# Second mixture: the second product by Strassen's algorithm in passes 1 and 2, with prepared weights kept in DRAM

## Chip, cores and metric

The kernel runs on one core of a Trainium2 chip. The metric is the device time of one execution in microseconds (us); lower is better. Engines are named TensorE (PE, its weight loads PEld), VectorE (DVE), ScalarE (ACT), GpSimd (POOL) and SyncE (SP, which issues nearly all DMAs here).

## The reference, cut to what matters

Attention with positive features gives x (2304 tokens by 512); a first mixture routes each token to one of 8 experts; the second mixture, below, sends every token through all 8 experts and weights them with a normalised gate P.

```python
def _moe2_ref(x, w_gate, w1, w2):          # x 2304x512, E = 8, F = 1024
    logits = x @ w_gate
    P = np.exp(logits - logits.max())
    for _ in range(8):
        P /= P.sum(1, keepdims=True) + 1e-09
        P /= P.sum(0, keepdims=True) + 1e-09
        P *= N / E
    out = np.zeros((N, D))
    for e in range(E):
        h = np.maximum(x @ w1[e], 0.0)
        out += P[:, e:e + 1] * (h @ w2[e])
    return out
```

## The kernel before

Attention and the first mixture come first; the second mixture (`moe2`) starts near 420 us of the span and is all that the change touches. Every fp32 operand is split into a high part, rounded to fp32r by ScalarE, and a low part, the rest, made by VectorE; a product is three matmuls, high by high, high by low and low by high.

The tokens are done in three passes of 768 (two halves of three 128-token tiles, `TB` = 3, `TW` = 384). In a pass the 8 experts' weights come in 16 parts of 512 hidden units; one part in one pass is a *quad*, 48 in all, 16 a pass, in reversed order every other pass. A quad has two groups (`group`, L1127), each for half of its hidden units.

The **first product** (x by w1) is done by Strassen's algorithm on 2x2 blocks: seven products for eight. `sums_w1` (L865) makes the sums of weight blocks on GpSimd, `w1_high` and `w1_low` (L879, L885) split the seven operands, `sum_x`, `x_high` and `x_low` do so for x once a pass. `mm` (L1069) issues one product: 6 matmuls of 384 columns. They add up in the PSUM tiles `pa`, `pb`, `pd` with a few VectorE sums (L1146, L1161, L1173), and `relu_high`, `relu_low` (L1087, L1095) leave the split activations.

The **second product** (activations by w2) is done plainly, a quad later: `piece` (L1101) takes one 128-token tile and issues 12 matmuls of 512 columns into `py`; VectorE multiplies by the gate and accumulates (L1123). `load_w2`, `w2_high`, `w2_low` (L1052 to L1065) bring the quad's four 128-row parts of w2 through two raw buffers. Weights are loaded, summed and split anew in every pass.

The gates are made in the first quads (`sinkhorn_start`, `sinkhorn_step`). From quad 3 (`AUTO`) on the order is the one written (`manual_schedule`, L1261): each engine runs its instructions in program order. `group` takes lists `high`, `low` and `fill`, which put the preparation of the next weights and the pieces of the quad before between the products. All loads and stores of `moe2` stand in the one SP queue, in program order.

Of the kernel before, what the change touches and what calls it, by code (L numbers as in the profile page):

```python
# [18 lines left out]
P = 128  # L19
# [794 lines left out]
def moe2(tc, nc, c, w_gate, w1, w2, x2d, xtd, out):  # L814
# [6 lines left out]
    with ExitStack() as ctx:  # L821
# [6 lines left out]
        ORDER = (1, 6, 7, 2, 5, 3, 4)  # L828
        AUTO = 3
        yield  # L830
        wp = ctx.enter_context(tc.tile_pool(name="m2w", bufs=1, reuse_waits="tile"))
        weights = [(e, q) for e in range(E) for q in range(NQ)]
        quads = []
# [9 lines left out]
        wc, wsrc = {}, {}  # L843

        def load_w1(m):

            if m >= len(wlist):
                return
            e, q = wlist[m]
            r = wp.tile([P, NKB, 2, QF], F32, name="r1", tag="r1")  # L850
            for h in range(2):
                nc.sync.dma_start(
                    r[:, :, h],
                    w1[e, :, 512 * h + QF * q : 512 * h + QF * q + QF].rearrange("(b p) f -> p b f", p=P),
                )
            wsrc[m] = r

        def views_w1(m):
            r = wsrc[m]
            a11, a12, a21, a22 = r[:, 0:2, 0], r[:, 2:4, 0], r[:, 0:2, 1], r[:, 2:4, 1]  # L860
            s1 = wp.tile([P, 2, QF], F32, name="s1", tag="s1")
            s2 = wp.tile([P, 2, QF], F32, name="s2", tag="s2")
            wsrc[m] = {1: a11, 6: s2, 2: a12, 7: a21, 5: s1, 3: a12, 4: a22}

        def sums_w1(m):  # L865
            if m:
                views_w1(m)
            a11, s2, a12, a21, s1, _, a22 = wsrc[m].values()
# [7 lines left out]
        def w1_tiles(m, k):  # L876
            wc[m, ORDER[k]] = [wp.tile([P, 2, QF], F32R, name=nm, tag=nm, bufs=7) for nm in ("wch", "wcl")]

        def w1_high(m, k):  # L879
            i = ORDER[k]  # L880
            if (m, i) not in wc:
                w1_tiles(m, k)
            nc.scalar.activation(wc[m, i][0], wsrc[m][i], AF.Copy)  # L883

        def w1_low(m, k):  # L885
            i = ORDER[k]
            src = wsrc[m]
            h, l = wc[m, i]
            nc.vector.tensor_tensor(l, src[i], f32(h), ALU.subtract)  # L889
            if i == 2 and m:  # L890
                nc.gpsimd.tensor_tensor(src[3], src[2], src[6], ALU.subtract)  # L891

        load_w1(0)
        views_w1(0)
        for k in range(7):
            w1_tiles(0, k)

        for k in (0, 3, 6, 1, 2, 4, 5):
            yield
# [27 lines left out]
        def load_x(t, tag="xr", bufs=2):  # L927
            xr = big.tile([P, D], F32, name="xr", tag=tag, bufs=bufs)
# [24 lines left out]
        def other_logits(ps_, h):  # L953
            xt = big.tile([P, NKB, TW], F32, name="xt", tag="xt")
            for i, t in enumerate(tiles(ps_, h)):
                transposed(load_x(t), lambda pt: [(xt[:, :, i * P : i * P + P], pt)])
# [11 lines left out]

        def new_x():
            for h in range(2):  # L970
                for kh in range(2):
                    xq[h, kh] = big.tile([P, 2, TW], F32, name="xq", tag="xq", bufs=4)
# [12 lines left out]
        xs, xc = {}, {}  # L985

        def sum_x(i, first=False):
            b11, b12, b21, b22 = xq[0, 0], xq[1, 0], xq[0, 1], xq[1, 1]
            v = nc.vector
            if i == 0:  # L990

                d = big.tile([P, NKB, TW], F32, name="xt", tag="xt")[:, 0:2] if first else b12
# [23 lines left out]
        def sum_4():  # L1016
            nc.vector.tensor_tensor(xs[4], xs[2], xs[6], ALU.subtract)
# [31 lines left out]
        hs = {}  # L1049
        w2s, w2r = {}, {}  # L1050

        def load_w2(m, b):  # L1052
            if m >= len(wlist):
# [15 lines left out]
        def mm(dst, n, g, i, start, stop):  # L1069
            wh, wl = wc[wid[n], i]  # L1070
            xh, xl = xc[i]
            sl = slice(g * P, g * P + P)
            m = 0
            for w, x in ((wh, xh), (wh, xl), (wl, xh)):
                for kb in range(2):
                    nc.tensor.matmul(  # L1076
                        dst, w[:, kb, sl], x[:, kb], start=(start and m == 0), stop=(stop and m == 5),
# [9 lines left out]
        def relu_high(n, g, half, which, src):  # L1087
            hh, hl = [
                big.tile([P, TW], F32R, name=f"{nm}{half}", tag=f"{nm}{half}", bufs=6 + 2 * half)
                for nm in ("hh", "hl")  # L1090
            ]
            nc.scalar.activation(hh, src, AF.Relu)  # L1092
            hs[n, 2 * g + which, half] = (hh, hl)
# [7 lines left out]
        def piece(n, half, i):  # L1101

            ps_, e, q = quads[n]
            k = n % len(weights)
# [3 lines left out]
            for b in range(4):  # L1108
                hh, hl = hs[n, b, half]
                wh, wl = w2s[wid[n], b]  # L1110
                for ht, wt in ((hh, wh), (hl, wh), (hh, wl)):
                    nc.tensor.matmul(py, ht[:, i * P : i * P + P], wt, start=(m == 0), stop=(m == 11))  # L1112
                    m += 1
            if k == 0:
                accs[t] = big.tile([P, D], F32, name="acc", tag="acc", bufs=2 * TB)
                if ps_ == 0:
                    nc.scalar.activation(accs[t], py, AF.Copy)
                else:
                    nc.scalar.activation(accs[t], py, AF.Copy, scale=lg[:, t, e : e + 1])
            elif k < NQ and ps_ == 0:  # L1120
# [3 lines left out]
            if k == len(weights) - 1:  # L1124
                nc.sync.dma_start(row(t, 1), accs[t])

        def group(n, g, fill, high, low, lead=()):  # L1127
# [16 lines left out]
            mm(b, n, g, 6, True, False)  # L1144
# [4 lines left out]
            mm(d, n, g, 7, True, False)  # L1149
# [8 lines left out]
            mm(b, n, g, 5, False, False)  # L1158
# [8 lines left out]
            mm(b, n, g, 3, False, True)  # L1167
            relu_high(n, g, 1, 0, b)
            relu_low(n, g, 1, 0, b)
            mm(d, n, g, 4, False, True)  # L1170
# [12 lines left out]
        xrs = [[load_x(t, "acc", 2 * TB) for t in tiles(0, h)] for h in range(2)]  # L1183
        for h in range(2):
            for i, t in enumerate(tiles(0, h)):
                x_block(xrs[h][i], h, i)
            if h == 0:
                xs.update({1: xq[0, 0], 2: xq[0, 1]})
                for k in (0, 3):
                    x_high(k)  # L1190
                    x_low(k, True)
        for i in range(3):
            sum_x(i, True)
            if i:
                x_high(i)
                x_low(i)
        sum_4()
        for k in (4, 5, 6):
            x_high(k)
            x_low(k)  # L1200
        others = [(ps_, h) for ps_ in range(1, NPASS) for h in range(2)]
        load_w2(0, 0)
        load_w2(0, 1)
# [166 lines left out]
```

## Time and profile before

| | before |
|---|---|
| three runs, us | 1963.07, 1967.33, 1971.89 (median 1967.33) |
| profiled execution, us | 1964.43 |
| its span, us | 1962.4, 32469 instructions |
| PE, DVE, ACT, POOL busy | 98%, 63%, 45%, 17% |
| mean granted clock of PE | 0.995 of full speed |
| DMA | 180.78 MB, mean 92 GB/s |

The span runs from the first to the last instruction; the rest of the profiled execution's time lies around it. Busy shares are of the whole span. A matmul's duration in the trace overlaps that of the next, so the distance between starts tells its rate.

### The profile page before, as it was taken

The numbers are of one execution on the slowest core, as the hardware profiler recorded it, in microseconds if no ns is written. First come the engines' busy times: TensorE is split into PE (matmuls) and PEld (weight loads), VectorE is DVE, ScalarE is ACT, GpSimd is POOL, SyncE is SP. The second block draws the span as 40 slices with busy tenths as digits, with TensorE's granted clock in tenths as the row PEclk, the third lists the DMA queues.
The fourth block names the chain that finished last, engine by engine and source line by source line (L and its number), as shares of the span: only waits on it lengthen the run. The fifth ranks groups of instructions, "written<-read, shape, count | busy, mean of one in ns | idle before, by whom it ended". The sixth has DMA issues, their size and how long they took to land.

```text
span 1962.4 us, 32469 instructions
## 1 busy us (share of the span) xinstructions
PE 1932.2 (98%) x12594; PEld 1732.4 (88%) x12594; DVE 1230.8 (63%) x2189; ACT 889.2 (45%) x1682; POOL 328.0 (17%) x294
## 2 busy tenths in 40 slices
PE   9999899989999999999999999999999999999999
PEld 8988889966889989899998989989998999999997
DVE  5777777764866656666655666565665656656563
ACT  5777555545444344344344434344444434444341
POOL 2011532211111111112021111111201111111110
PEclk9999999989999999999999999999999999999999
DMA  6324686545122121222122121222202122121211
GB/s 180 105 64 112 162 305 221 205 126 170 65 65 71 59 75 54 81 84 72 68 62 76 54 82 54 81 72 90 76 35 92 54 80 73 56 76 54 83 47 43
DMA packets 132550, 180.78 MB, mean 92 GB/s; under 512 B 22370, under 2 KB 86114, under 8 KB 132384
## 3 DMA queue, kind: packets, MB, share of 16 engines
q1 hardware_dynamic: 128768, 171.22, 28.4%
q0 software_dynamic: 3456, 7.30, 1.0%
q8 instruction: 101, 1.65, 0.4%
q14 instruction: 65, 0.53, 0.1%
q10 hardware_dynamic: 160, 0.07, 0.0%
HBM read 163.85 MB, written 17.15 MB: 92 GB/s over the span
## 4 chain that ended last, share of the span: by engine, by line
PE 77%; DVE 0%; DMA 0%; ACT 0%; issue 0%; SPq 0%; ACTq 0%
PE py L1112 40%; PE pb L1076 15%; PE pa L1076 10%; PE pd L1076 10%; PE pg L944 1%; PE pt L936 1%; DMA xr<-x2d 0%; ACT acc L1260 0%; DVE w2l L1067 0%; PE pl L949 0%; PE pc L1042 0%; DVE lg L1047 0%; DVE hl L1097 0%; DVE cs L1040 0%; DVE wcl L889 0%
## 5 line engine op out<-in xcount | busy, mean ns | idle before, releaser
L1112 PE MATMUL py<-w2h,hh 128*128 128x512 f32 x1152 | 452.1, 392 | 0.0
L1112 PE MATMUL py<-w2l,hh 128*128 128x512 f32 x1152 | 451.7, 392 | 0.0
L1112 PE MATMUL py<-w2h,hl 128*128 128x512 f32 x1152 | 449.8, 390 | 0.0
L1123 DVE SCALAR_TENSOR_TENSOR acc<-py,lg,acc 128x512 f32<-128x512 f32 x264 | 197.6, 748 | 156.0 <-PE py L1112 155.1
L1112 PEld LDWEIGHTS py<-w2l,hh 128*128 128x128 f32 x1152 | 216.1, 188 | 50.2 <-issue 1.3
L1112 PEld LDWEIGHTS py<-w2h,hl 128*128 128x128 f32 x1152 | 216.3, 188 | 37.2
L1112 PEld LDWEIGHTS py<-w2h,hh 128*128 128x128 f32 x1152 | 216.4, 188 | 35.6
L1067 DVE TENSOR_TENSOR w2l<-r,w2h 128x512 fp32r<-128x512 f32 x184 | 129.3, 704 | 73.3 <-ACT w2h L1062 73.3
L891 POOL TENSOR_TENSOR r<-r,s 128x512 f32<-128x512 f32 x45 | 58.2, 1293 | 685.8 <-DVE wcl L889 685.8
L1092 ACT ACTIVATE hh<-c 128x384 fp32r<-128x384 f32 x192 | 101.0, 526 | 129.4 <-DVE c L1161 65.3
L1084 ACT ACTIVATE z<-pb 128x384 f32<-128x384 f32 x96 | 47.1, 490 | 246.3 <-PE pb L1076 246.2
L889 DVE TENSOR_TENSOR wcl<-r,wch 128x512 fp32r<-128x512 f32 x230 | 154.0, 685 | 2.5 <-ACT wch L883 2.3
L870 POOL TENSOR_TENSOR s<-r 128x512 f32<-128x512 f32 x46 | 59.7, 1298 | 569.1 <-DMA r<-in_moe_w_dram 569.1
L1076 PE MATMUL pb<-xch,wch 128*128 128x384 f32 x576 | 148.3, 338 | 1.1 <-ACT z L1084 1.1
L1076 PE MATMUL pb<-xcl,wch 128*128 128x384 f32 x576 | 147.8, 337 | 0.0
L1076 PE MATMUL pb<-xch,wcl 128*128 128x384 f32 x576 | 147.4, 337 | 0.0
L1084 ACT ACTIVATE s<-pa 128x384 f32<-128x384 f32 x96 | 47.1, 491 | 212.8 <-PE pa L1076 212.7
L883 ACT ACTIVATE wch<-r 128x512 fp32r<-128x512 f32 x230 | 138.7, 622 | 7.8 <-PE pd L1076 3.0
L1146 DVE TENSOR_TENSOR pb<-pb,s 128x384 f32<-128x384 f32 x96 | 54.3, 565 | 131.4 <-ACT wch L883 63.1
L1076 PEld LDWEIGHTS pb<-xch,wch 128*128 128x128 f32 x576 | 106.5, 188 | 17.2 <-ACT z L1084 2.3
L1062 ACT ACTIVATE w2h<-r 128x512 fp32r<-128x512 f32 x184 | 114.1, 621 | 3.8 <-DMA r<-in_moe_w_dram 3.6
L1097 DVE SCALAR_TENSOR_TENSOR hl<-c,hh 128x384 fp32r<-128x384 f32 x192 | 106.4, 554 | 6.2 <-ACT hh L1092 6.1
(241 smaller groups left out, 3557.3 us busy)
## 6 DMA issues: line engine op xcount, KB each, us to landing
r<-in_moe_w_dram SPq DMA_DIRECT2D x168, 512.0 KB
r<-in_moe_w_dram SPq DMA_DIRECT2D x184, 256.0 KB
qt<-in_q_dram SPq DMA_DIRECT2D x16, 288.0 KB
x2d<-x SPq DMA_DIRECT2D x4, 1152.0 KB
xr<-x2d SPq DMA_DIRECT2D x18, 256.0 KB
out_dram<-acc SPq DMA_DIRECT2D x18, 256.0 KB
kt<-in_k_dram SPq DMA_DIRECT2D x16, 256.0 KB
vs<-in_v_dram SPq DMA_DIRECT2D x14, 256.0 KB
```

The costliest lines, as they stand in the source:

```text
L870: g.tensor_tensor(s1, a21, a22, ALU.add)
L883: nc.scalar.activation(wc[m, i][0], wsrc[m][i], AF.Copy)
L889: nc.vector.tensor_tensor(l, src[i], f32(h), ALU.subtract)
L891: nc.gpsimd.tensor_tensor(src[3], src[2], src[6], ALU.subtract)
L1062: nc.scalar.activation(h, w2r[m, b], AF.Copy)
L1067: nc.vector.tensor_tensor(l, w2r.pop((m, b)), f32(h), ALU.subtract)
L1076: nc.tensor.matmul(dst, w[:, kb, sl], x[:, kb], start=(start and m == 0), stop=(stop and m == 5), skip_group_check=True,)
L1084: nc.scalar.activation(t, src, AF.Copy)
L1092: nc.scalar.activation(hh, src, AF.Relu)
L1097: nc.vector.scalar_tensor_tensor(hl, src, 0.0, f32(hh), ALU.max, ALU.subtract)
L1112: nc.tensor.matmul(py, ht[:, i * P : i * P + P], wt, start=(m == 0), stop=(m == 11))
L1123: nc.vector.scalar_tensor_tensor(accs[t], py, lg[:, t, e : e + 1], accs[t], ALU.mult, ALU.add)
```

## The change

In pass 0 the second product stays as it was. In passes 1 and 2 it is done by Strassen's algorithm too, and transposed: w2 is the stationary side, the activations move, and the result has the features on the partitions. As the gate of a token then runs along the free axis, it is multiplied into the activations (`h_of`: maximum with 0, times the gate) before they are split. Seven operands for w2 are prepared in pass 0 and stored in DRAM (`wd2`), with the four sums-based operands of w1 (`wd1`); passes 1 and 2 load them. The gates go to DRAM as well (`ptd`) and come back spread over the partitions. The results are turned back by TensorE at the end of a pass (`out_tile`, `turn_part`).

In pass 0, added to each quad:

```diff
+        def sums_w2(m):
+            g = nc.gpsimd
+            x, y = sum_tiles(m)[0]
+            b11, b21 = w2r[0][:, 0:QF], w2r[0][:, QF:D]
+            b12, b22 = w2r[1][:, 0:QF], w2r[1][:, QF:D]
+            g.tensor_tensor(x[:, 0], b21, b22, ALU.add)
+            g.tensor_tensor(x[:, 1], x[:, 0], b11, ALU.subtract)
+            g.tensor_tensor(y[:, 0], b11, b21, ALU.subtract)
+            g.tensor_tensor(y[:, 1], b12, x[:, 1], ALU.subtract)
+        def sums_low(m, i, g):
+            raw, t = sum_tiles(m)
+            nc.vector.tensor_tensor(t[:, 1], raw[i], f32(t[:, 0]), ALU.subtract)
+            for j, op in enumerate(((5, 6), (7, 3))[i]):
+                nc.sync.dma_start(wd2[op][m][:, :, g], f32(t[:, :, j]))
+        def store_w2(m, g):
+            t, u = w2s[m, 2 * g], w2s[m, 2 * g + 1]
+            for op, src in ((1, t[:, :, 0:QF]), (2, u[:, :, 0:QF]), (4, u[:, :, QF:D])):
+                nc.sync.dma_start(wd2[op][m][:, :, g], f32(src))
+        def store_w1(m, i):
+            nc.sync.dma_start(wd1[i][m], f32(wc[i]))
```

In passes 1 and 2 a quad is 14 slots. In slot s TensorE does one of the 14 products of the first product (`first`) and then one unit of the second product of the quad before (`unit`, 6 matmuls of 384 columns); `flush` adds the unit to one of seven accumulators, five times in 14 by ScalarE and GpSimd, else by VectorE. A list of events with times in slots, sorted, gives every engine's order:

```diff
+        def unit(i, k):
...
+            pu = st["pu", k] = ps.tile([P, TW], F32, name="pu", tag="YT"[k % 2], bufs=2)
...
+            for wl, xl in ((0, 0), (0, 1), (1, 0)):
+                for kb in range(2):
+                    nc.tensor.matmul(
+                        pu, w[:, wl, kb, g2 * P : g2 * P + P], H[:, hx[kb][xl].start + o], start=(m == 0), stop=(m == 5)
+                    )
...
+        def flush(i, k):
...
+            elif k in GFL:
+                tmp = temps[GFL.index(k) % 2]
+                nc.scalar.activation(tmp, pu, AF.Copy)
+                nc.gpsimd.tensor_tensor(t, t, tmp, ALU.add)
+            else:
+                nc.vector.tensor_tensor(t, pu, t, ALU.add)
...
+                for s in range(14):
+                    at(B0 + s, first, n, s // 7, s % 7)
+                    if n > NW:
+                        at(B0 + s + 0.5, unit, i - 1, s)
+                        at(B0 + s + 1.02, flush, i - 1, s)
...
+                    at(t + 2.52, lambda n=n, g=g: h_of(n, 0, 0, st["pa", g]))
+                    at(t + 3.2, high, "A", g)
+                    at(t + 3.45, low, "A", g)
+                    at(t + 3.55, zcopy, g)
+                    at(t + 3.9, c22, g)
+                    at(t + 4.0, lambda n=n: h_of(n, 1, 2, st["z"]))
...
+                    at(t + 5.8, tt, G, R[:, 6:8], R[:, 1:3], R[:, 0:2], ALU.subtract)
...
+                    e = 14.1 if g == 0 else 9.2
+                    at(t + e, high, "D", g)
+                    at(t + e + 0.5, low, "D", g)
```

Highs and lows A and B are of 384 elements, C of 768, D of 1152. Per quad there are seven 512 KB loads of w2's operands, four of w1's, and three raw parts of w1 of 256 KB, which are split as before. Between passes 1 and 2 (`turn`) x is summed on GpSimd and split again, and seven adds of 768 combine the accumulators, five of them on VectorE; at the end there are seven more, five on GpSimd.

**TensorE, one stretch of pass 1.** Before, twelve matmuls of 512 columns (`py`) follow a product (`pb`, two matmuls a row):

```order
L1076 MATMUL pb<-xch,wch 128x384 x2
L1076 MATMUL pb<-xcl,wch 128x384 x2
L1076 MATMUL pb<-xch,wcl 128x384 x2
L1112 MATMUL py<-w2h,hh_11792 128x512
L1112 MATMUL py<-w2h,hl_11793 128x512
L1112 MATMUL py<-w2l,hh_11792 128x512
```

and after, product and unit alternate (`hh` is the tile of all split activations, `w_8478` that of the loaded operands of w2):

```order
L1118 MATMUL pb<-xch_8491,wc_3599 128x384 x2
L1118 MATMUL pb<-xcl_8492,wc_3599 128x384 x2
L1118 MATMUL pb<-xch_8491,wc_3599 128x384 x2
L1357 MATMUL pu<-hh,w_8478 128x384 x6
L1118 MATMUL pa<-xch_8483,wc_3595 128x384 x2
```

The 512-column matmuls are gone from these passes; each product is followed by six of 384.

**VectorE, the same stretch after the change.** `acc<-pu,acc` are flushes, `hr<-` gated activations, `hh<-hr,hh` lows, `z<-pd,z` and `c<-pd,v` the first product's sums:

```order
L1396 SCALAR_TENSOR_TENSOR hr<-pa,acc 128x384
L1372 TENSOR_TENSOR acc<-pu,acc 128x384
L882 TENSOR_TENSOR wc_3596<-r_3592,wc_3596 128x512
L1404 TENSOR_TENSOR hh<-hr,hh 128x384
L1413 TENSOR_TENSOR z<-pd,z 128x384
L1396 SCALAR_TENSOR_TENSOR hr<-z,acc 128x384
L1372 TENSOR_TENSOR acc<-pu,acc 128x384
L1404 TENSOR_TENSOR hh<-hr,hh 128x384
L1396 SCALAR_TENSOR_TENSOR hr<-pb,acc 128x384
L1417 TENSOR_TENSOR c_17328<-pd,v 128x384
L1372 TENSOR_TENSOR acc<-pu,acc 128x384
L1404 TENSOR_TENSOR hh<-hr,hh 128x768
```

The gate has moved from the 512-wide accumulation into `hr`, and accumulations and lows stand in one line with the sums that free the first product's PSUM.

**SP, one quad of pass 0.** Before, a quad's loads (`r`) stand alone:

```order
L1058 DMA r_12115<-in_moe_w_dram 128x512
L1058 DMA r_12117<-in_moe_w_dram 128x512
L852 DMA r_12262<-in_moe_w_dram 128x4x256 x2
L1058 DMA r_12292<-in_moe_w_dram 128x512
L1058 DMA r_12306<-in_moe_w_dram 128x512
```

and after, part of the quad's 18 stores (`wd_`) stands among them:

```order
L1072 DMA acc<-in_moe_w_dram 128x512 x2
L1111 DMA wd_116<-w_8482 256x1x256
L1111 DMA wd_117<-w_8478 256x1x256
L1111 DMA wd_119<-w_8478 256x1x256
L887 DMA wd_112<-wc_3600 128x1024
L887 DMA wd_113<-wc_3601 128x1024
L1106 DMA wd_120<-acc 256x1x256
L1106 DMA wd_121<-acc 256x1x256
L887 DMA wd_114<-wc_3599 128x1024
L887 DMA wd_115<-wc_3597 128x1024
L1106 DMA wd_122<-acc 256x1x256
L1106 DMA wd_118<-acc 256x1x256
```

The next loads of w1 and w2 now stand behind these stores in the same queue.

## Rows read from the trace of the kernel before

**Rows 1.** The page, parts 1 and 4: busy time; chain that ended last.

```profile
PE 1932.2 (98%) x12594; PEld 1732.4 (88%) x12594; DVE 1230.8 (63%) x2189; ACT 889.2 (45%) x1682; POOL 328.0 (17%) x294
...
PE 77%; DVE 0%; DMA 0%; ACT 0%; issue 0%; SPq 0%; ACTq 0%
PE py L1112 40%; PE pb L1076 15%; PE pa L1076 10%; PE pd L1076 10%; PE pg L944 1%; PE pt L936 1%; DMA xr<-x2d 0%; ACT acc L1260 0%; DVE w2l L1067 0%; PE pl L949 0%; PE pc L1042 0%; DVE lg L1047 0%; DVE hl L1097 0%; DVE cs L1040 0%; DVE wcl L889 0%
```

**Rows 2.** Windows: us, busy PE, PEld, DVE, ACT, POOL, granted clock, DMA share, GB/s.

```profile
640.00:1110.00 470.00, 470.00 (x2351) 424.63 (x2350) 283.95 (x460) 195.94 (x380) 73.70 (x57) 1.00 0.22 70
```

**Rows 3.** Chain in order of time, pass 1: start, us, what.

```profile
1050.29 2.76 PE py L1112 x12
...
1065.89 2.76 PE py L1112 x12
```

**Rows 4.** Timeline of TensorE, pass 1: first of 24, first of 12, next.

```profile
1006.09 0.51 PE L1076 MATMUL pa<-xch,wch 128*128 128x384 f32 x2
...
1010.28 0.40 PE L1112 MATMUL py<-w2h,hh 128*128 128x512 f32 x1
...
1013.02 0.51 PE L1076 MATMUL pb<-xch,wch 128*128 128x384 f32 x2
```

**Rows 5.** Groups by form, second mixture and whole span: busy, mean ns.

```profile
L1161 DVE TENSOR_TENSOR c<-pd,z 128x384 f32<-128x384 f32 x84 | 46.8, 557 | 77.5 <-ACT z L1084 77.5
...
L889 DVE TENSOR_TENSOR wcl<-r,wch 128x512 fp32r<-128x512 f32 x195 | 130.4, 685 | 0.0
...
L1012 DVE TENSOR_TENSOR xcl<-xq,xch 128x768 fp32r<-128x768 f32 x8 | 7.6, 950 | 2.7 <-ACT xch L1006 2.7
...
L1123 DVE SCALAR_TENSOR_TENSOR acc<-py,lg,acc 128x512 f32<-128x512 f32 x245 | 183.4, 749 | 145.7 <-PE py L1112 145.6
...
L1084 ACT ACTIVATE z<-pb 128x384 f32<-128x384 f32 x84 | 41.3, 491 | 229.0 <-PE pb L1076 229.0
...
L870 POOL TENSOR_TENSOR s<-r 128x512 f32<-128x512 f32 x46 | 59.7, 1298 | 569.1 <-DMA r<-in_moe_w_dram 569.1
...
L273 POOL TENSOR_TENSOR lall<-lall 128x324 f32<-128x324 f32 x1 | 0.9, 873 | 6.5 <-DVE lall L257 6.5
```

**Rows 6.** Timeline at the change from pass 0 to 1: start, us, engine.

```profile
917.36 1.29 POOL L870 TENSOR_TENSOR s<-r 128x512 f32<-128x512 f32 x1 [12.31 <-DMA r<-in_moe_w_dram]
...
917.88 1.60 DVE L993 TENSOR_TENSOR xq<-xq 128x768 f32<-128x768 f32 x1
...
918.74 1.89 POOL L871 TENSOR_TENSOR s<-s,r 128x512 f32<-128x512 f32 x1
...
919.51 1.93 DVE L997 TENSOR_TENSOR t<-xq 128x768 f32<-128x768 f32 x1
...
920.59 2.01 POOL L872 TENSOR_TENSOR r<-r 128x512 f32<-128x512 f32 x1
```

**Rows 7.** Timeline of VectorE and GpSimd, pass 1.

```profile
1043.61 1.29 POOL L871 TENSOR_TENSOR s<-s,r 128x512 f32<-128x512 f32 x1
1044.42 0.75 DVE L1123 SCALAR_TENSOR_TENSOR acc<-py,lg,acc 128x512 f32<-128x512 f32 x1 [1.66 <-PE py L1112]
```

**Rows 8.** Windows: stores of x2d; loads of w1; stores and loads mixed.

```profile
212.00:215.00 3.00, 2.88 (x25) 2.68 (x23) 3.00 (x11) 2.15 (x7) 0.00 (x0) 1.00 1.03 341
...
1008.00:1010.00 2.00, 2.00 (x13) 2.00 (x13) 1.15 (x2) 1.35 (x3) 0.00 (x0) 1.00 1.06 374
...
215.00:216.00 1.00, 0.28 (x3) 0.07 (x1) 1.00 (x6) 1.00 (x3) 0.00 (x0) 1.00 1.02 206
```

**Rows 9.** Windows: quads 1 and 2.

```profile
490.00:540.00 50.00, 49.65 (x252) 44.19 (x251) 42.42 (x109) 22.32 (x43) 6.78 (x5) 1.00 0.19 64
```

**Rows 10.** Timeline of TensorE in the first mixture: four transposes.

```profile
256.48 0.63 PE L666 MATMUL pt<-ident,xg 128*128 128x128 f32 x4 [0.76 <-DMA xg<-x2d,ix]
```

**Rows 11.** Timeline at the end: the last matmul.

```profile
1958.18 0.39 PE L1112 MATMUL py<-w2l,hh 128*128 128x512 f32 x1
```

**Rows 12.** Groups of weight loads, 640 to 1960 us: busy, mean ns.

```profile
L1076 PEld LDWEIGHTS pb<-xch,wch 128*128 128x128 f32 x500 | 93.1, 188 | 12.7
```

More of the change, by code (lines that the diff above doesn't have):

```diff
@@ L811, in moe1, with moe2 @@
     yield
-def moe2(tc, nc, c, w_gate, w1, w2, x2d, xtd, out):
+def moe2(tc, nc, c, w_gate, w1, w2, x2d, xtd, wd1, wd2, ptd, out):
     with ExitStack() as ctx:
@@ L1203, in moe2, with both, f @@
         load_w2(0, 1)
-        def quad(n):
-            ps_, e, q = quads[n]
-            nxt = n + 1 < NQD and quads[n + 1][0] != ps_
-            near = n + 4 < NQD and quads[n + 4][0] != ps_ and quads[n + 3][0] == ps_
-            fresh = n == 0 or wid[n] != wid[n - 1]
-            more = n + 1 < NQD and wid[n + 1] != wid[n]
+        for i in (6, 7, 5, 3):
+            store_w1(0, i)
+        def both(*fs):
+            def f():
+                for g in fs:
+                    g()
+            return f
+        def quad(n):
+            more = n + 1 < NW
             for g in range(2):
@@ L1230, in quad, with lo @@
-                    if nxt:
+                        sums_w1(n + 1)
+                    for b, k in enumerate((0, 1, 4, 5)):
+                        high[k] = lambda b=b: w2_high(n, b)
+                        def lo(b=b):
+                            w2_low(n, b)
+                            if b < 2:
+                                load_w2(n, b + 2)
+                        low[k] = lo
+                    if not more:
                         for i, k in enumerate((2, 3, 6)):
                             low[k] = lambda i=i: sum_x(i)
+                    low[3] = both(low[3], lambda: store_w2(n, 0))
@@ new lines, in copy_b, with h_of, high, low @@
+        def copy_b(g):
+            nc.scalar.activation(new("pb", g, 2), st["pa", g], AF.Copy)
+        def h_of(n, half, u, src):
+            b = st["gate", n]
+            nc.vector.scalar_tensor_tensor(R[:, u], src, 0.0, gates[:, b, half], ALU.max, ALU.mult)
+        def high(nm, g):
+            hx, u, v = raws[nm]
+            nc.scalar.activation(H[:, hx[g][0]], R[:, u:v], AF.Copy)
+        def low(nm, g):
+            hx, u, v = raws[nm]
+            nc.vector.tensor_tensor(H[:, hx[g][1]], R[:, u:v], f32(H[:, hx[g][0]]), ALU.subtract)
@@ new lines, in vcopy, with zcopy, c22, c21 @@
+        def vcopy():
+            st["v"] = copied(st["pb", st["g"]], "v", "v")
+        def zcopy(g):
+            st["z"] = copied(st["pb", g], "z", "sz")
+        def c22(g):
+            nc.vector.tensor_tensor(st["z"], st["pd", g], st["z"], ALU.add)
+        def c21(g):
+            t = st["c"] = big.tile([P, TW], F32, name="c21", tag="cc")
+            nc.vector.tensor_tensor(t, st["pd", g], st["v"], ALU.add)
+        def load_gate(r):
+            ps_, e, _ = quads[NW + 2 * r]
+            for h in range(2):
+                t = tiles(ps_, h)[0]
+                src = ptd[e * NT + t : e * NT + t + TB].rearrange("t p -> (t p)")
+                nc.sync.dma_start(gates[:, r % 2, h], src.partition_broadcast(P))
@@ L1261, in moe2, with at, tt @@
         with tc.manual_schedule():
-            for n in range(AUTO, NQD):
+            for n in range(AUTO, NW):
                 quad(n)
-            for h in range(2):
-                for i in range(TB):
-                    piece(NQD - 1, h, i)
+            top.close()
+            R = side("m2b").tile([P, 8, TW], F32, name="hr")
+            ev = []
+            def at(t, f, *a):
+                ev.append((t, len(ev), f, a))
+            def tt(eng, out_, a, b, op=ALU.add):
+                eng.tensor_tensor(out_, a, b, op)
@@ L1328, in routed @@
             route(0, psum)
[L1330 removed]
+    m2 = moe2(tc, nc, c, moe2_w_gate, moe2_w1, moe2_w2, x2d, xtd, wd1, wd2, ptd, out)
     next(m2)
```

427 lines of the change are left out of this document (304 added, 123 removed).

## The prediction

> **What bounds the kernel now.** I read the page first, for shares: TensorE is busy 98% of the span and the chain that ended last is TensorE for 77%, with the second product (`py`, L1112) at 40% and the three accumulators of the first product (`pb`, `pa`, `pd`, L1076) at 35% [rows 1]. Shares do not say which stage has slack, so next came the windows. From 640 to 1110 us TensorE has no idle time, at granted clock 1.00, while VectorE is at 60% (283.95 of 470), ScalarE at 42%, GpSimd at 16% and the DMA engines at 0.22 with 70 GB/s [rows 2]. The chain in order of time gives the period: the same piece comes back every 15.60 us, twice a quad, so a quad is 31.2 us [rows 3]. The second mixture after its start is 48 such quads, and only its TensorE time counts, as long as the others keep up.
>
> **Removed and added on TensorE.** A matmul's mean duration (337 and 392 ns) overlaps its neighbours, so it is no price; the distance between starts is. From 1006.09 to 1010.28 there are 24 matmuls of 384 columns: 4.19 us, 0.1746 each; the 12 of 512 columns behind them take 2.74 us [rows 4]. A quad's first product is 7 x 2 x 6 = 84 matmuls of 384 columns: 14.67 us. The rest of 31.2, 16.53 us, is its second product, 6 pieces x 12 = 72 matmuls of 512 columns (0.230 each). In passes 1 and 2 the change puts 14 units x 6 = 84 matmuls of 384 columns there: again 14.67 us, so a quad falls to 29.33 us. 32 quads x 1.87 = **-59.8 us**. Seven products for eight are worth less than an eighth here, because a column costs more in the narrower matmul.
>
> **Do the other engines fit in 29.33 us?** Prices per instruction are in [rows 5]: VectorE 0.557 us for 384 elements, 0.685 for 512, 0.950 for 768; for 1152 I estimate 1.35 by their slope. A quad of pass 1 or 2 then holds on VectorE 9 flushes, 8 gated activations (`h_of`), 4 lows of 384 and 4 sums `c22`/`c21` (25 x 0.557), 2 lows of 768 (1.90), 2 of 1152 (2.70), 3 weight lows (2.06): 20.6 us. ScalarE: 11 copies (0.49), 4 + 2 + 2 highs and 3 weight highs, some 14 us. GpSimd, at 0.873 us for 324 elements and 1.30 for 512: nine instructions of 384 (1.01) and two of 768 (1.9): 12.9 us. Each fits alone.
>
> But two of them share something. At 917.36 a GpSimd add starts; the VectorE subtract that starts inside it takes 1.60 us and the next one 1.93, where the same shape takes 0.95, and the GpSimd instructions between them take 1.89 and 2.01 instead of 1.30 [rows 6]: they take turns. At 1044.42, though, a VectorE accumulation that reads PSUM and SBUF runs inside a GpSimd instruction at its usual 0.75 us [rows 7]. The subtract that waits has both inputs in SBUF. So I count as exclusive GpSimd's 12.9 us and VectorE's instructions with two SBUF inputs: 15 a quad, the eight lows (6.8), four of the gated activations (2.2), the weight lows (2.06), 11.1 us. Together 24.0 us of 29.33. VectorE itself: if each of the 15 finds GpSimd busy with its share of time (44%) and waits half of an instruction (0.65), that is 4.3 us, in all 24.9 us, 85%. I take no TensorE wait in the steady quads, with 0 as one end of the range and 1.5 us a quad as the other.
>
> The Trainium skill says this as a rule that speaks against the change ("SBUF — State Buffer", section "SBUF: two separate sides"): VectorE and GpSimd share a port pair that is an exclusive lock held for the whole instruction, and a VectorE instruction without a faster mode takes it only when it has two SBUF inputs, against a GpSimd instruction that reads SBUF. The trace agrees for the subtract (1.60 and 1.93 against 0.95 us) and for the accumulation (0.75). By the rule the sum stays 24.0 us a quad; if every VectorE instruction were shut out, as one may read [rows 6] without the accumulation, it would be 20.6 + 12.9 = 33.5 and TensorE would wait.
>
> **DMA.** In pass 0 a quad now issues 18 stores (4 of 512 KB, 14 of 256 KB) beside its 6 loads: 5.8 + 2.1 = 7.9 MB in 31.2 us, 252 GB/s. Stores of 1 KB rows to DRAM ran at 341 GB/s and loads of 1 KB rows at 374 when the engines were full [rows 8]; at 341 the quad's transfers take 23 us. All stand in one SP queue, so a `load_w2` waits behind stores, and a store behind VectorE's low; slack is half a quad. I take +2 us for quads 3 to 15 (0 to 20: half a GpSimd instruction each at the least, 1.5 us each at the most). Passes 1 and 2 move 6.7 MB in 29.3 us, 229 GB/s, in 4 KB rows mostly, six slots ahead: hidden.
>
> Quads 0 to 2 have less cover: from 490 to 540 us VectorE is already at 42.42 of 50 [rows 9], with the gates' normalisation; four 512-wide lows a quad (2.7 us) and eight 256-wide GpSimd sums (some 0.7 us each, 5.6 in all, which shut out lows) come on top. **+5 us** (0 to 10). The four stores of the first prepared weights, 2.1 MB, fall into the first mixture's loads: 6.2 us at that rate if nothing hides it. They come once, and weights there are loaded a slot of work ahead: **+1** (0 to 6).
>
> **The edges.** Start of pass 1: VectorE's 20.6 us and six old accumulations (0.749) make 25.1 in that quad, before waits: **+3** (0 to 6). Between passes 1 and 2 three quads carry 7 lows of 768 and 5 adds of 768 more on VectorE (11.4 us, less 2.1 of weight lows), and 4 + 2 of 768 on GpSimd (11.4): 20.7 us of exclusive time where the steady quad leaves 5.3, and 24 transposes, four in 0.63 us [rows 10], 3.8 us. The adds and the PSUM banks that transposes share with the units come in one bunch, so I choose near the upper end: **+17** (4 to 24). At the end, the accumulation and the last transfer now take 4.0 us behind TensorE (last matmul started 1958.18, span 1962.4) [rows 11]; then come two adds, 24 transposes, copies and the last three transfers, some 7.5. In the last 14 units (14.67 us) GpSimd has five adds of 768 (9.5 us) that VectorE's adds and so the PSUM buffers wait for: **+13** in all (4 to 20).
>
> **Sum:** -59.8 + 2 + 5 + 1 + 3 + 17 + 13 = -18.8 us. The profiled execution took 1964.43 us, so 1945.6; the median of the three runs (1963.07 to 1971.89) is 2.9 above it, so **1948 us** for the median.
>
> **Rivals.**
> *Cheaper edges.* The transitions overlap with TensorE after all: 4 + 4 + 1 instead of 33 leaves -59.8 + 8 + 9 = -43: 1924. For it: TensorE hid every bunch of the kernel before, the sums at 917 among them. Against it: three quads over their exclusive budget.
> *VectorE and GpSimd lead the steady quad (slower).* At the place where `c22` and `h_of` free PSUM for the next product, a wait behind a GpSimd instruction of 1.9 us reaches TensorE in every quad. The forecast has 18.8 us to lose and there are some 31 such quads, so 0.6 us a quad eats all of it and 0.9 makes it slower by over 0.5%; at 1.5 us it is 1948 + 46 = 1994. For it: 85% on an engine that waits in order. Against it: 5.3 us of room, and instructions that stand slots away from their consumers.
> *Stores bind pass 0.* If these stores moved at 230 GB/s (one full microsecond among x2d's stores and loads shows 206 [rows 8]), 7.9 MB would take 34.3 us, +3.1 in each of 13 quads: 1948 + 38 = 1986. Against it: 341 GB/s.
> *No gain on TensorE.* If a weight load of 188 ns [rows 12] set the distance, 84 would cost 15.8 us and the quad save only 0.74: 1948 + 36 = 1984. Against it: 0.1746 is measured between 384-wide matmuls that each load weights.
>
> **Chances.** Forecast 0.50 (its own range 1932 to 1960), cheaper edges 0.18, VectorE and GpSimd leading 0.17, stores 0.12, no gain 0.03. A measurement of this kernel can tell about 0.5%, 9.8 us. Faster by more (below 1957.5): 0.46 of the forecast's 0.50, 0.18, and 0.04 of milder forms of the two next, 0.68. Within it: 0.04, and 0.12 of these two, 0.16. Slower: the rest, 0.16. The range from 1918 to 1976 leaves out some 0.04 below and 0.16 above.
>
> **What would show it.** In the profile after: TensorE's period in pass 1 near 29.3 us at clock 1.00 with no idle in front of L1357 or L1118; units at 0.1746 us a matmul; VectorE near 70% to 85% there with its two-input subtracts stretched; idle TensorE bunched at the change of passes and after the last first product; DMA share under 0.9 in pass 0, and its quads still 31.2 us. A period above 30 us in pass 1 with TensorE waiting for VectorE, or a pass 0 longer than before by over 20 us, would make the forecast wrong.

## The result, and the profile after

The median of four runs after the change is 1946.16 us (1944.32 to 1951.20), of four runs before it 1966.92; the ratio is 0.990, with a 95% interval of 0.987 to 0.993. The forecast was 1948. The profiled execution took 1944.32 us. Its page, against [rows 1]:

```profile
span 1942.6 us, 34972 instructions
...
PE 1892.5 (97%) x13028; PEld 1781.2 (92%) x13028; DVE 1347.6 (69%) x2309; ACT 931.5 (48%) x1679; POOL 747.1 (38%) x652
```

Windows (columns as in [rows 2]) of pass 0, pass 1, the change to pass 2, and the end:

```profile
640.00:900.00 260.00, 259.95 (x1294) 234.09 (x1293) 184.53 (x291) 123.31 (x241) 96.24 (x98) 1.00 0.73 255
...
1100.00:1300.00 200.00, 200.00 (x1145) 200.00 (x1144) 137.98 (x220) 87.34 (x151) 94.61 (x74) 1.00 0.70 230
1380.00:1500.00 120.00, 116.53 (x671) 115.32 (x670) 87.91 (x123) 58.35 (x105) 66.12 (x44) 1.00 0.62 210
1880.00:1943.00 63.00, 49.98 (x278) 49.00 (x276) 36.36 (x56) 17.33 (x28) 31.11 (x22) 0.94 0.37 117
```

In the steady passes TensorE has no idle time. Between 1380 and 1500 us, which hold the change from pass 1 to 2 (the *turn*), it is idle for 3.5 of 120 us, and at the end for 13 of 63. The chain in order of time answers to [rows 3]: a unit takes 1.04 us and a product 1.06, 0.175 us a matmul.

```profile
1104.45 1.04 PE pu L1357 x6
1105.49 1.06 PE pb L1118 x6
1106.55 1.04 PE pu L1357 x6
```

ScalarE's first copy of `pa` marks a half of a quad. In the timeline after the change, the start of quad 3, of quad 4, of quad 16, and three halves of pass 1:

```profile
544.51 0.49 ACT L1126 ACTIVATE s<-pa 128x384 f32<-128x384 f32 x1 [2.44 <-PE pa L1118]
...
582.44 0.49 ACT L1126 ACTIVATE s<-pa 128x384 f32<-128x384 f32 x1 [1.76 <-PE pa L1118]
...
959.47 0.47 ACT L1392 ACTIVATE pb<-pa 128x384 f32<-128x384 f32 x1 [0.56 <-PE pa L1118]
...
1104.48 0.47 ACT L1392 ACTIVATE pb<-pa 128x384 f32<-128x384 f32 x1 [0.50 <-PE pa L1118]
1119.18 0.47 ACT L1392 ACTIVATE pb<-pa 128x384 f32<-128x384 f32 x1 [0.50 <-PE pa L1118]
1133.88 0.47 ACT L1392 ACTIVATE pb<-pa 128x384 f32<-128x384 f32 x1 [0.50 <-PE pa L1118]
```

and the first three before it:

```profile
537.50 0.49 ACT L1084 ACTIVATE s<-pa 128x384 f32<-128x384 f32 x1 [2.58 <-PE pa L1076]
...
570.60 0.49 ACT L1084 ACTIVATE s<-pa 128x384 f32<-128x384 f32 x1 [2.23 <-PE pa L1076]
...
945.27 0.49 ACT L1084 ACTIVATE s<-pa 128x384 f32<-128x384 f32 x1 [2.08 <-PE pa L1076]
```

A steady quad is 1133.88 - 1104.48 = 29.40 us (forecast 29.33). By stage:

| stage of the profiled executions | before | after | difference | forecast |
|---|---|---|---|---|
| up to quad 0 | 429.6 | 429.5 | -0.1 | +1 |
| quads 0 to 2 | 107.9 | 115.0 | **+7.1** | +5 |
| quads 3 to 15 | 407.8 | 415.0 | **+7.2** | +2 |
| quad 16 to the end | 1017.1 | 983.1 | **-34.0** | -26.8 |
| span | 1962.4 | 1942.6 | -19.8 | -18.8 |

Quad 3 alone takes 33.1 us before and 37.9 after. So quads 0 to 3 together, as the experiments take them, are 141.0 and 152.9 (+11.9), and quads 4 to 15 are 374.7 and 377.0 (+2.4). The total agrees, but the terms behind it were off and cancelled. The experiments ask whether VectorE and GpSimd really take turns, and how near the steady quad is to being bound by that; what the 11.9 us are; and what the edges hold.

### The profile page after: what moved, and what is told of

The parts are those of the page before. It is cut to its first block, busy times and chain, and to the rows that moved or that the text cites. A ratio compares the mean times of both kernels' runs of the same rounds, so it can differ in the third digit from the quotient of the medians.

```text
span 1942.6 us, 34972 instructions
## 1 busy us (share of the span) xinstructions
PE 1892.5 (97%) x13028; PEld 1781.2 (92%) x13028; DVE 1347.6 (69%) x2309; ACT 931.5 (48%) x1679; POOL 747.1 (38%) x652
## 4 chain that ended last, share of the span: by engine, by line
PE 68%; DVE 3%; POOL 1%; DMA 1%; issue 1%; ACT 1%; SPq 0%; POOLq 0%; DVEq 0%; ACTq 0%
PE pu L1357 23%; PE pb L1118 14%; PE py L1153 12%; PE pd L1118 9%; PE pa L1118 9%; POOL acc L1447 1%; POOL hr L1447 0%; DVE hh L1404 0%; DMA acc<-in_moe_w_dram 0%; DVE hh L1139 0%; DVE wc L882 0%; DVE xcl L1016 0%; DMA w<-wd 0%; DVE acc L1372 0%; DVE hr L1396 0%
## 5 line engine op out<-in xcount | busy, mean ns | idle before, releaser
L1357 PE MATMUL pu<-hh,w 128*128 128x384 f32 x2688 | 540.4, 336 | 8.0 <-DVE acc L1447 4.2
L1357 PEld LDWEIGHTS pu<-hh,w 128*128 128x128 f32 x2688 | 473.4, 188 | 9.5 <-DVE acc L1447 4.6
L1447 POOL TENSOR_TENSOR hr<-hr 128x384 f32<-128x384 f32 (+1 forms) x192 | 282.3, 1470 | 289.2 <-DVE hr L1396 166.5
L1118 PE MATMUL pb<-xch,wc 128*128 128x384 f32 x1152 | 297.8, 339 | 1.7 <-ACT v L1126 0.6
L1153 PE MATMUL py<-w,hh 128*128 128x512 f32 x1152 | 287.5, 396 | 0.0
L1404 DVE TENSOR_TENSOR hh<-hr,hh 128x384 fp32r<-128x384 f32 (+2 forms) x256 | 223.1, 881 | 62.8 <-ACT hh L1400 61.5
L1153 PEld LDWEIGHTS py<-w,hh 128*128 128x128 f32 x1152 | 215.4, 189 | 43.1 <-issue 1.9
L1118 PEld LDWEIGHTS pb<-xch,wc 128*128 128x128 f32 x1152 | 210.1, 188 | 9.6 <-ACT v L1126 1.5
L1118 PE MATMUL pa<-xch,wc 128*128 128x384 f32 x768 | 198.8, 338 | 0.1
L1118 PE MATMUL pd<-xch,wc 128*128 128x384 f32 x768 | 197.4, 338 | 0.3 <-DVE c L1211 0.2
```

What stands on the lines that cost most here:

```text
L1118: nc.tensor.matmul(dst, wc[i][:, w, kb, sl], xcb[i][x][:, kb], start=(start and m == 0), stop=(stop and m == 5), skip_group_check=True,)
L1153: nc.tensor.matmul(py, ht[:, i * P : i * P + P], w[:, wt], start=(m == 0), stop=(m == 11))
L1357: nc.tensor.matmul(pu, w[:, wl, kb, g2 * P : g2 * P + P], H[:, hx[kb][xl].start + o], start=(m == 0), stop=(m == 5))
L1404: nc.vector.tensor_tensor(H[:, hx[g][1]], R[:, u:v], f32(H[:, hx[g][0]]), ALU.subtract)
L1447: eng.tensor_tensor(out_, a, b, op)
```

## Experiments

Each was profiled beside the kernel before (1966.4 to 1968.1 us). Quads 0 to 2 are ordered automatically and differ by some us from run to run, so most comparisons are made from quad 4 to the end: 1360.2 us after the change.

**How many flushes GpSimd takes: 14, none, 9 (the change: 5).**

```diff
-        GFL = (3, 5, 8, 10, 12)
+        GFL = tuple(range(14))
```

> All 14 flushes of a quad of passes 1 and 2 go by ScalarE and GpSimd, none by VectorE (the change has 5 of 14). Theory, taking turns: an instruction of GpSimd and one of VectorE with two inputs in SBUF never run together. GpSimd's 12.9 us a quad become 12.9 + 9 x 1.08 = 22.6, VectorE's two-input instructions stay at 11.1, so 33.7 us must fit one behind the other: the quad of 29.4 grows to at least 33.7, 31 quads by 4.3 or more, the time to about 2080 us or above, and TensorE waits before the units. Rival, each engine by itself: GpSimd 22.6, VectorE 15.6, ScalarE 18.5 of 29.4 us all fit, the quad stays at 29.4 and the time at 1946 plus or minus 4.

2016.33 us: a steady quad of 31.2 us, between the two theories. Windows, and then groups by form of VectorE, 1100 to 1300:

```profile
1100.00:1300.00 200.00, 191.71 (x1082) 187.95 (x1081) 127.92 (x148) 98.37 (x199) 167.06 (x130) 1.00 0.66 222
```
```profile
L1404 DVE TENSOR_TENSOR hh<-hr,hh 128x384 fp32r<-128x384 f32 x26 | 25.4, 976 | 20.6 <-ACT hh L1400 20.6
L882 DVE TENSOR_TENSOR wc<-r,wc 128x512 fp32r<-128x512 f32 x19 | 22.6, 1191 | 0.0
...
L1396 DVE SCALAR_TENSOR_TENSOR hr<-c,acc 128x384 f32<-128x384 f32 x13 | 14.7, 1129 | 0.4
...
L1396 DVE SCALAR_TENSOR_TENSOR hr<-pb,acc 128x384 f32<-128x384 f32 x13 | 7.2, 551 | 0.0
L1417 DVE TENSOR_TENSOR c<-pd,v 128x384 f32<-128x384 f32 x13 | 7.1, 547 | 0.0
```

The same groups after the change, and gated activations with both inputs in SBUF (`hr<-z`):

```profile
L882 DVE TENSOR_TENSOR wc<-r,wc 128x512 fp32r<-128x512 f32 x21 | 16.8, 801 | 0.0
L1404 DVE TENSOR_TENSOR hh<-hr,hh 128x384 fp32r<-128x384 f32 x28 | 15.5, 552 | 0.0
...
L1396 DVE SCALAR_TENSOR_TENSOR hr<-z,acc 128x384 f32<-128x384 f32 x14 | 9.9, 704 | 1.0
...
L1417 DVE TENSOR_TENSOR c<-pd,v 128x384 f32<-128x384 f32 x14 | 7.8, 558 | 17.4 <-PE pd L1118 17.4
```

Only instructions with both inputs in SBUF got longer (552 to 976 ns, 801 to 1191); those that read PSUM stay at 547 to 558 beside a GpSimd that is busy 84% of the time. That the two take turns is shown by this. That it is what makes the quad 1.8 us longer is argued only. VectorE is busy less than after the change (127.92 of 200 us), so its own work is not the limit. What TensorE and ScalarE wait for in the same window is:

```profile
PE pb L1118 <- ACT z L1126: 8.3, 6, 1.4
```
```profile
ACT hh L1400 <- POOL hr L1447: 38.7, 12, 3.9
ACT s L1369 <- POOL acc L1370: 35.2, 27, 2.1
```

TensorE waits for a copy of ScalarE, and ScalarE, whose instructions run in program order, for subtracts and flushes of GpSimd. So the longer way of a flush, over two engines in line, is a rival, and no run separates it from the taking of turns. The count was too strict in any case, 33.7 us for 31.2.

```diff
-        GFL = (3, 5, 8, 10, 12)
+        GFL = ()
```

> All 14 flushes on VectorE, none by ScalarE and GpSimd. Theory, taking turns with room left: exclusive time falls from 24.0 to 12.9 - 5 x 1.08 + 11.1 = 18.6 us a quad, VectorE's own rises to 20.6 + 2.8 = 23.4 and with fewer waits to some 26 of 29.4; the quad stays at 29.4 and the time at 1946 plus or minus 4. Rival, VectorE's in-order stream is what the quad hangs on and the five flushes on GpSimd are what keeps it at 29.4: the quad grows by a good part of 2.8 us, to 30 us or more, the time to 1965 or more.

1939.67 us: the steady quad stays at 29.40, as the theory has it, though the time fell by more than it allowed: 1353.7 us from quad 4 on, 6.5 less. The gain lies at the edges, the long quad at the turn (36.54 to 33.17 us) and the end (66.6 to 63.7 us from the start of quad 47). The windows show VectorE at 76% and GpSimd at 29%:

```profile
1100.00:1300.00 200.00, 200.00 (x1145) 200.00 (x1144) 151.33 (x254) 70.62 (x117) 58.38 (x40) 1.00 0.70 233
```

With `GFL = (1, 3, 4, 5, 7, 8, 10, 11, 12)`:

> 9 of 14 flushes by ScalarE and GpSimd (5 after the change; 14 gave a quad of 31.2, none 29.4). Theory, turns, with the count scaled to the 14-flush run (31.2 measured for 33.7 counted): 24.0 + 4 x 1.08 = 28.3 counted, 26.2 scaled, still below 29.4: the quad stays at 29.4, and only the change of passes and the end get dearer, by 2 to 6 us in all: 1950. Rival: a steep threshold, where any more work on GpSimd reaches TensorE: 30 us or more a quad, above 1962.

1956.72 us. The quad is 29.40, so there is no threshold near; from quad 4 on it is 1368.5, 8.3 more, at the turn and the end, dearer than expected. (The rest of the time lies ahead of quad 4.)

**Pass 0 without its stores.**

```diff
+                if m == NW - 1:
                     nc.sync.dma_start(wd2[op][m][:, :, g], f32(src))
```

and so for the other two kinds of store.

> All stores of prepared weights are left out but those of the last part, and passes 1 and 2 load that part every time (the preparation itself stays; the output is of that one part). Theory: the stores' traffic slows every second quad of pass 0 (31.58 us instead of 31.22); without them all are at 31.2, quads 4 to 15 lose 2.4 us, the time is about 1943.5. Rival 1: the slowing comes from the added work on GpSimd or from where the tiles lie in SBUF, and the 31.58 stay; 1946. Rival 2: the stores in the SP queue also hold up the loads of quads 1 to 3; then those give back several of their 11.9 us more than before the change, and the time is below 1940.

1952.65 us. Rival 1 holds (which of its two causes is not shown): from 4 to 15 the quads still alternate, 31.22 and 31.58, 376.7 us in all (377.0), at 72 GB/s instead of 255. So the stores cost quads 4 to 15 at most 0.3 us. The automatic order of quads 0 to 2 came out otherwise and took longer (158.8 us for quads 0 to 3), so rival 2 could not be judged.

**Parts 0 to 2 not prepared.** `sums_w2`, `sums_high`, `sums_low`, `store_w2` and `store_w1` return for `m < 3`.

> For parts 0 to 2 the sums, splits and stores for passes 1 and 2 are left out, and those passes load part 3 in their place (so the output has wrong weights for three parts). The gates' store stays. Theory: two causes in quads 1 to 3, which took 11.9 us more than before the change. GpSimd's sums of w2 wait for tiles that the transposes of the other passes' x still use, the sums of w1 stand behind them, and ScalarE's highs behind those: quad 1 returns from 40.9 to about 37 us and quad 2 from 36.1 to about 33.5. The gates' store causes what is left in quad 3: it stays at 36.5 to 38 (33.1 before the change). In all 6 to 8 us less, 1939. Rival: all of it is the added preparation and quad 3 falls to 33 too, 1934. Other rival: the automatic order of quads 0 to 2 came out worse and nothing returns, 1946.

1940.94 us; quads 0 to 3 take 36.0, 43.7, 32.8 and 34.8 us. Quad 2 returns to its time before the change (32.9). Quad 3 is only 0.8 us below the runs with 14, none and 9 flushes on GpSimd (35.55 to 35.65). Quad 1 doesn't return; in the new order TensorE waits 2.9 us for a load of x2d and the granted clock is 0.79 there. The three theories are not told apart for quad 1.

**The gates' store later, with its own buffers.**

```diff
-            lt = big.tile([P, E, NT], F32, name="lt", tag="v")
+            lt = Z[:, 5120 : 5120 + E * NT].rearrange("p (e t) -> p e t", e=E)
...
+                if n == AUTO:
+                    store_gates()
```

> The gates' store gets buffers of its own (it shared the buffer of the copies v of the first product) and stands behind quad 3, in the part whose order is written by hand, where its inputs have long been ready. Theory: in quad 3 TensorE's transposes wait for the copy lt, and the copies v wait until the gates' DMA has read the shared buffer; without both, quad 3 takes 33 to 34 us (33.1 before the change; 37.9 after it with 3.4 us of that at a lower granted clock behind the waits, 35.5 in the two runs with other flushes). Rival: quad 3 is late for the automatic order of the quads ahead, and stays at 35 to 36. Quads 1 and 2 are ordered anew, so only quad 3 is compared.

Quad 3 took 33.77 us, as the theory has it (1949.74 us in all, as quads 0 to 2 came out in a slower order). In the change's profile TensorE waits there for `lt` and works at a lower clock behind; in another run of the same order (`tail_v` below) the clock stayed. Windows, first after the change:

```profile
550.00:558.00 8.00, 6.21 (x19) 4.96 (x20) 4.40 (x7) 6.13 (x12) 2.17 (x2) 0.65 0.19 51
558.00:566.00 8.00, 8.00 (x37) 6.91 (x37) 5.85 (x9) 2.93 (x6) 3.17 (x4) 0.92 0.49 168
```

then of `tail_v`:

```profile
550.00:558.00 8.00, 4.98 (x23) 3.71 (x23) 4.46 (x8) 5.89 (x11) 4.02 (x3) 1.00 0.15 44
558.00:566.00 8.00, 8.00 (x40) 7.01 (x39) 6.89 (x13) 3.40 (x7) 2.13 (x3) 1.00 0.60 198
```

Quad 3 is 37.9 us in the one and 35.7 in the other: 2.3 us are the clock, some 2 the shared buffer and the place. The kernel without GpSimd flushes, profiled twice, shows the same: 35.63 us at clock 1.00 and 37.95 with a fall to 0.63 in the same window.

**The turn: sums of x on VectorE.**

```diff
-                        at(B0 - 13 + 3 * k, sum_x, k, False, G)
+                        at(B0 - 13 + 3 * k, sum_x, k, False, V)
...
-                    at(B0 + 10.6, sum_4, G)
+                    at(B0 + 10.6, sum_4, V)
```

> Between passes 1 and 2 the four sums of x of 768 elements go to VectorE instead of GpSimd. Theory, turns of two-input instructions: GpSimd gives 4 x 2.0 us and VectorE takes 4 x 0.96, so the adds that the transposes wait for (2.6 us) come earlier; the long quad at the change of passes falls from 36.5 to 33 to 34 us (33.2 without flushes on GpSimd), the time by 2 to 3 us to 1943. Rival: VectorE's own queue is what is late there, 3.9 us more in it make the quad 38 or more and the time 1948.

Neither: the long quad stays at 36.71 us, and so does TensorE's wait for the adds (2.7 us); 1949.99 us. A wait of 0.9 us for a copy is gone, but here the granted clock falls to 0.62 behind the wait, so that two transposes, a unit and a product take 3.92 us:

```profile
1468.44 0.44 PE L1431 MATMUL pt<-ident,acc 128*128 128x128 f32 x2 [0.37 <-DVE acc L1447]
...
1472.36 0.60 PE L1431 MATMUL pt<-ident,acc 128*128 128x128 f32 x4
```

instead of 2.38 after the change:

```profile
1462.35 0.44 PE L1431 MATMUL pt<-ident,acc 128*128 128x128 f32 x2 [0.37 <-DVE acc L1447]
...
1464.73 0.60 PE L1431 MATMUL pt<-ident,acc 128*128 128x128 f32 x4
```

So the run shows that the sums of x don't make the wait for the adds; without the lower clock its long quad would have been some 35.2 us. What the transposes wait for is seen in the timeline of VectorE, GpSimd and TensorE after the change:

```profile
1455.79 2.88 POOL L1370 TENSOR_TENSOR acc<-acc,s 128x384 f32<-128x384 f32 x2
...
1456.84 0.96 DVE L1447 TENSOR_TENSOR acc<-acc 128x768 f32<-128x768 f32 x1 [2.13 <-POOL acc L1370]
...
1461.57 0.41 PE L1431 MATMUL pt<-ident,acc 128*128 128x128 f32 x2 [2.20 <-DVE acc L1447]
```

A flush on GpSimd, behind two of its other instructions, holds VectorE's first add, that add the three others in line (with a weight low of 1.50 us between them), and these the transposes. Without flushes on GpSimd this wait is gone and the turn costs 3.77 us, about its transposes.

**The end: three adds on VectorE** (`M1` to `M7` are the seven accumulators).

```diff
-            at(B0 + 6.1, tt, G, M3, M3, M5)
-            at(B0 + 6.2, tt, G, M3, M3, M6)
+            at(B0 + 6.1, tt, V, M3, M3, M5)
+            at(B0 + 6.2, tt, V, M3, M3, M6)
...
-            at(B0 + 8.3, tt, G, M4, M4, M7)
+            at(B0 + 8.3, tt, V, M4, M4, M7)
```

> At the end three adds of 768 (M3 += M5, M3 += M6, M4 += M7) go from GpSimd to VectorE. They took 6.96 us on GpSimd with 1.7 and 0.7 us of waits for them on VectorE; on VectorE they are 3 x 0.95. Theory: TensorE's wait of 4.2 us for the accumulators before the last two units falls below 1 us, the end comes 3 to 5 us earlier, 1942. Rival: VectorE then reaches the last five adds later by itself, and the wait stays within 1 us of 4.2; 1946.

1943.97 us. The wait fell from 4.2 to 2.2 us and the end from 66.6 to 65.1, half of what the theory gave: the adds on VectorE now wait 2.7 us for a flush on GpSimd. The two ends are not at one clock: here it falls one wait earlier, and the 36 matmuls behind that wait take 8.1 us instead of 6.5.

**A better version.** First the kernel without GpSimd flushes, timed:

> The kernel without flushes on ScalarE and GpSimd again, now timed against the kernel before. From quad 4 to the end its profile took 6.5 us less than that of the change (1353.7 against 1360.2). Theory: this is no chance of one profile, and the ratio to the kernel before falls by 0.003 from 0.990 to 0.986 to 0.988, some 1941 us. Rival: the two profiles differ by where the clock fell in quads 0 to 3, and the ratio stays at 0.989 to 0.991.

1940.41 us, ratio 0.9866 (0.9847 to 0.9884), as the theory has it. This interval overlaps that of the change (0.9867 to 0.9927); that the gain is no chance of one profile rests on the stretch from quad 4 on: 1352.8 us here and 1353.7 in the first profile, against 1359.7 to 1362.3 in the six profiles with five flushes on GpSimd.

> All flushes on VectorE; the gates' store with buffers of its own, where it was; and another end: the adds M3, M4, M5, M7 on VectorE, the last unit pair added once into M7 ahead of M5 += M7 and M4 += M7 (instead of into both), the last gated activations ahead of lows C, and three of the six last outputs sent from free tiles so that none waits for an earlier transfer. Theory: the end's cost is made of waits for adds (2.6 + 2.4 us of TensorE in the run without GpSimd flushes) and of 2 us in which the fifth and sixth copies wait for the DMAs of the first, not of the 24 transposes; from the start of quad 47 to the end 63.7 us fall to 55 to 58, quad 3 by 0 to 2 more, the time to 1933 plus or minus 4, ratio 0.981 to 0.985. Rival: the last matmul, the transposes and one transfer set the end, and at most the 2 us of the copies come back: 1938.

1932.84 us, ratio 0.9834 (0.9814 to 0.9854): 61.0 us from quad 47 to the end, more than expected, and quad 3 at 33.35. This version computes its last quad wrongly, so its time doesn't count; the next one mends that.

> As the run before, but the last quad's second half keeps three of its activations in the tile of raw w1, which is free by then; in the run before they overwrote tiles that the first half had not yet split, so it computed that quad wrongly. Theory: time is unchanged by that or a little less, as VectorE no longer splits the first half late: from the start of quad 47 to the end 59 to 61 us (66.6 after the change, 61.0 in the run before), ratio 0.981 to 0.985, about 1932. Rival: VectorE's work itself, not the waits, fills the last 20 us, and the end stays at 61 or more, 1934.

1936.44 us, ratio 0.9847 (0.9833 to 0.9860). Quad 47 to the end is 60.5 us; TensorE's waits there fell to 2.3 us, none longer than 0.8, and the granted clock stays at 1.00 until the last transpose. What is left follows from VectorE's chain of adds.

```diff
-                    if more:
-                        sums_w1(n + 1)
...
+                    if more:
+                        sums_w1(n + 1)
+                    if n < AUTO:
+                        sums_w2(n)
```

> As best2, and in quads 0 to 2 GpSimd's sums of w1 are put ahead of its sums of w2. Theory: after the change GpSimd stood idle for 24 us in front of the sums of w2, whose tiles the other passes' x still used, and the sums of w1 behind them held up ScalarE's highs of the next weights and the logits behind those; with the order turned, quad 1 falls from 40.9 by 2 to 4 us (36.9 before the change) and the time by as much, 1929. Rival: quad 1 is late for the loads of x and the waits of the gates' work, and the automatic order comes out otherwise but no shorter: quads 0 to 3 together stay at 148 to 153 us.

1936.18 us, ratio 0.9837 (0.9823 to 0.9852): the same. Its profile has 152.4 us for quads 0 to 3, with a wait of 7.2 us for a load of x2d, as the rival says. The last two versions beat the kernel of the change, whose interval (0.9867 to 0.9927) lies above theirs.

## Why the prediction was right, and where it was wrong

The mechanism of the steady passes came out as forecast. That the total agrees within 1 us is luck: the turn was 9.9 us cheaper than its term, and the columns (2.2 us), quads 0 to 2 (2.1) and quads 3 to 15 (5.2) were dearer.

**Columns.** -59.8 was forecast, 32 x (31.2 - 29.40) = -57.6 came: the distance between matmuls is 0.1750 us and not 0.1746. The rival in which a weight load of 188 ns sets the distance is out; weight loads fill the steady passes (200.00 of 200 us) and still overlap.

**Steady waits.** 0, as chosen; VectorE and GpSimd don't lead. The runs with other flushes show the margin: 9 of 14 on GpSimd still cost the steady quad nothing, 14 cost 1.8 us. The sum of 24.9 us for VectorE was too high, its busy time is 137.98 x 29.4 / 200 = 20.3 us, waits included. The step that failed is that each two-input instruction would meet GpSimd at random; GpSimd's subtracts are released by VectorE's own results, and the lows of 384 ran undisturbed (552 ns); only weight lows (801 ns for 685 before the change) and the gated activations `hr<-z` (704 for 557) met it in part. GpSimd's groups after the change, 1100 to 1300 us, show whom it waited for:

```profile
L1447 POOL TENSOR_TENSOR hr<-hr 128x384 f32<-128x384 f32 x26 | 31.0, 1193 | 18.7 <-DVE hh L1404 17.7
L1447 POOL TENSOR_TENSOR hr<-hr 128x768 f32<-128x768 f32 x14 | 28.5, 2034 | 30.0 <-DVE hr L1396 30.0
```

That the two meet less often for it is argued from these rows, not shown. The Trainium skill ("SBUF — State Buffer", section "SBUF: two separate sides") has VectorE's instructions without a faster mode and with at most one input in SBUF run beside a busy GpSimd, and those with two shut out while it reads SBUF; the runs agree (551 against 976 and 1129 ns). Taken as exclusive for whole durations, as the Trainium skill has it, the 14-flush quad would need 33.7 us at the prices of the expectation, which is an estimate; 31.2 were measured, and the measurement decides.

**Pass 0.** The +2 was for quads 3 to 15, which took +7.2; 4.8 of it is quad 3. In quads 4 to 15 it is +2.4, near the forecast by luck and not for the reason given. Stores are hidden (376.7 and 377.0 us at 72 and 255 GB/s); every second quad is 0.36 us longer, with and without them. The Trainium skill (the same section) has DMA ports and engine ports apart, so that neither slows the other, and this run agrees.

**Quads 0 to 3.** For quads 0 to 2, +5 (0 to 10) against +7.1, all of it in quads 1 and 2; the two better versions whose clock stayed there (best and best2) have +7.2 and +5.6. Quad 2 returns without the added preparation; what makes quad 1 longer stays open. Quad 3 was mis-sized: its +4.8 are the lower clock (some 2.3 us) and the gates' store with its shared buffer (some 2), and the sum had neither.

**The turn: mis-sized.** +17 against 36.54 - 29.40 = +7.1. The step that failed is "three quads over their exclusive budget": it took time that VectorE and GpSimd lack for time of TensorE. Quads 30 to 32, in which the sums and splits of x run, took 29.40 to 29.41 us, so there the lack reached TensorE not at all. What reached it, in quad 33, is the transposes (some 3.6 us) and 3.5 us of waits (2.6 for the adds, 0.9 for a copy); taking the sums of x from GpSimd left the wait for the adds as it was.

**Start of pass 1 and end.** What remains of -34.0 after -57.6 and +7.1 is +16.5, against +3 and +13. At the start of pass 1 TensorE waits 1.0 us in all (940 to 1010 us), so most of it is the end. There its waits are, after the change:

```profile
PE pu L1357 <- DVE acc L1447: 4.2, 1, 4.2
PE pu L1357 <- DVE acc L1372: 2.5, 1, 2.5
```

and behind the longer one, the last, the granted clock falls to 0.50. Windows, and the last two units in the chain:

```profile
1928.00:1932.00 4.00, 2.82 (x9) 2.82 (x10) 3.38 (x7) 0.00 (x0) 0.53 (x1) 0.50 0.02 4
1932.00:1936.00 4.00, 4.00 (x24) 3.90 (x23) 1.24 (x3) 0.72 (x2) 0.00 (x0) 0.65 0.00 0
```
```profile
1929.18 4.21 PE pu L1357 x12
```

The transposes start at 1933.18, so these 12 matmuls take 4.0 us instead of 12 x 0.175 = 2.1: 1.9 us are the clock, which the sum did not have. Then come 24 transposes (3.6 us, in part at the lower clock) and the last copies and transfers, up to 1942.6. The clock falls in the last units in the profile of every run with this end, and in none of the three better versions, where no wait is longer than 1.1 us.

**Rivals.** The stores don't bind pass 0. A steady quad gets longer only with all 14 flushes on GpSimd, and then by 1.8 us. The cheaper edges were half right: the turn was, the end wasn't, and quads 0 to 15 took back most of what the turn left.

## What to carry to other kernels

A steady stage is safe where the engines that share something have a margin, and then relief for one of them is worth nothing there, while its longer way (two engines instead of one) can cost at the edges: look there for who waits for the helper. Work over an engine's budget for a few quads is not yet idle time of the bound engine; price the chain that ends in the bound engine's next instruction. A buffer shared with a rare DMA belongs on the list of waits. A wait of the bound engine can cost twice, once as idle time and once as a lower clock behind it: here 4.2 us at the end were followed by 1.9 more.

## Not expected

Every second quad of pass 0 is slower by 1.2% (31.58 against 31.22 us) with no idle time at granted clock 1.00, in every run after the change and in none before. A matmul of 512 columns starts 233.2 ns after its neighbour instead of 229.2, one of 384 176.1 instead of 175.2, and leaving out the stores doesn't change that. The added work of GpSimd and VectorE is the same in every quad of pass 0; where the tiles lie differs between even and odd parts. That this is the cause wasn't tried.

Runs of one kernel differ by up to 9 us. Part of it shows in the profiles of the change and its variants: in quads 0 to 3 the granted clock falls, in other places from run to run, to means of 0.63 to 0.9 over 8 us (between the levels of 1.2 and 2.4 GHz). In the windows above TensorE was idle longer (3.0 of 8 us) in the run that kept 1.00 than in that which fell to 0.65 (1.8 of 8 us), so idle time in those windows alone doesn't tell which run falls.
